# Four product groups of two Mish blocks made inside the pairs' stage before them

## The chip, the cores and the metric

The kernel runs on one core of a Trainium2 chip. The time is that of one launch on the device, in microseconds (us). A core has five engines that run side by side, each through its own list of instructions in order: TensorE (PE, matmuls, with its weight loads PEld), VectorE (DVE), ScalarE (ACT), GpSimd (POOL) and SyncE (SP, which here only issues DMAs). They wait for one another through semaphores.

## The reference

Attention with one added to the softmax's denominator, then a feed-forward layer with Mish:

```python
scores = scale * np.matmul(q, k.transpose(0, 1, 3, 2))      # (8, 12, 448, 448)
m = np.max(scores, axis=-1, keepdims=True)
e = np.exp(scores - m)
attn = e / (np.sum(e, axis=-1, keepdims=True) + np.exp(-m) + 1e-09)
attn_out = np.matmul(attn, v)                               # (8, 12, 448, 64)
x = attn_out.transpose(0, 2, 1, 3).reshape(3584, 768)
h = x @ w_in                                                # (3584, 2048)
sp = np.where(h > 20.0, h, np.log1p(np.exp(np.minimum(h, 20.0))))
g = h * np.tanh(sp)                                         # Mish
out = g @ w_out                                             # (3584, 768)
```

All inputs and the output are float32 in memory; the kernel computes with bfloat16 operands.

## The kernel before

Two heads make a *pair*, a batch has six pairs (`HP`), so there are 48, and three pairs make a *unit*. Units 0 and 1 (pairs 0 to 5, batch 0) run in a loop of their own (line 635). The loop at line 670 runs the units 2 to 15, and then four more rounds without attention. Each of its rounds has two parts:

- The **pairs' stage**, twelve steps `n`, four for each pair. A step makes two tiles of exponentials with row sums on ScalarE (`exps`, line 353), and then fills the three score tiles `sc_tiles` again: score matmuls on TensorE, then the negated row maximum on VectorE (`scores`, line 307). So the scores run three steps ahead of the exponentials. From unit 4 on, pieces of the second product (`mm2_part`, line 539) are laid between the steps. In units 2 and 3 there are none yet: TensorE transposes scores, spreads denominators, and at step 7 makes six matmuls on a constant tile (`keep_busy`, dummies, line 745), whose result nobody reads.
- The **Mish block**, eight groups `f`. Each group is six product matmuls x·w_in (`mm1_mish`, line 509) into one PSUM bank and a Mish on ScalarE into `gT`. The unit 2 block makes the groups 0 to 7 of batch 0, unit 3 the groups 8 to 15, and so on. ScalarE loads a table before the Mishes and again before the next exponentials. Between the groups, the next unit's q and k are transposed (`transpose_pair`) and taken out of PSUM (`evac_qk`), and after group 7 its first three scores are issued. These have to find their PSUM banks empty.

The product groups use the two banks `mo_tiles` in turn, and the third group of a block takes a half of `sc_tiles[0]`. The same two banks serve the spreads and the transposes on TensorE.

A pair's exponentials `en` go through these steps:

1. `denominators` (line 379): den and its reciprocal `rden` on VectorE, for the three pairs of a unit together, after a last small exponential `expm` of the maxima; for pairs 0 to 11 also a split of `rden` in two bfloat16 parts `hl` on GpSimd.
2. Either `normalise` divides `en` on VectorE (seven instructions, line 430; pairs from 12 on, `LATE_DIV`), or, for pairs 0 to 11, the division is made after the product with v: `spread_rden` (line 394) brings the reciprocals into a row layout by 16 small matmuls and a copy `rb`, and the result is multiplied by `rb` on its way from PSUM to `xT` (line 493).
3. `en` is transposed to `eT`, by a DMA that SyncE issues (line 438), or on TensorE (`turn_on_pe`, line 443) for the pairs 5, 6 and 7 (`BY_PE`) and for the last quarter of the first six.
4. `av_pair` (line 461) multiplies by v, into half a score tile, and its result goes to `xT[b]`, the operand of the product groups. `AV_AT` gives the steps for pairs 3 to 8; from pair 9 on the product of pair p lies ahead of the last scores of pair p + 3.

`RDEN_AT` says at which step of units 2, 3 and 4 a pair's denominators are spread. The matrices `w_in` (12 pieces) and `w_out` (8 pieces) are loaded by DMAs that GpSimd issues (`load_w`, line 160), at the steps in `W_AT` and at three places outside it. With `behind=p`, a small copy that reads pair p's `eT` goes ahead, so that GpSimd waits for that transpose. GpSimd also casts q, k and v (`cast`), in the same order of instructions.

For pairs from 12 on, q is laid out in two diagonal blocks (`q_diag`, four buffers), whose other halves are zeros. They are set once for each buffer, for pairs 12 to 15 (lines 264 and 265, VectorE).

The order of all this is written out by hand (`manual_schedule`): each engine runs its instructions in program order.

## Time and profile before

| | us |
|---|---|
| three runs | 473.57, 473.69, 466.44 |
| median of them | 473.57 |
| profiled execution, its time | 468.53 |
| profiled execution, its span (first to last instruction) | 466.8 |

| engine | busy us | share of the span | instructions |
|---|---|---|---|
| TensorE | 449.8 | 96% | 3051 |
| VectorE | 344.1 | 74% | 657 |
| ScalarE | 332.8 | 71% | 877 |
| GpSimd | 180.4 | 39% | 258 |

The mean granted TensorE clock of the profiled execution is 0.985 of full speed. The loop of units 0 and 1 ends near 46 us, units 2 and 3 take the time to 97.4 us, and all that comes after lasts to 466.8 us. A product matmul of 448 columns shows 352 ns from its start to its end, but starts follow each other faster than that, since matmuls are pipelined; where the cost of a row of them matters, it is read from the time that a whole group took.

How to read the lines below: each stands for one instruction, or for several of the same kind in a row (x8), with its start and length in us, its engine, the line of the kernel, and "what it writes<-what it reads". In square brackets is the time that the engine sat idle before, and what ended it.

### The profile page before, as it was taken

The numbers are of one execution on the slowest core, as the hardware profiler recorded it, in microseconds if no ns is written. First come the engines' busy times: TensorE is split into PE (matmuls) and PEld (weight loads), VectorE is DVE, ScalarE is ACT, GpSimd is POOL, SyncE is SP. The second block draws the span as 40 slices with busy tenths as digits, with TensorE's granted clock in tenths as the row PEclk, the third lists the DMA queues.
The fourth block names the chain that finished last, engine by engine and source line by source line (L and its number), as shares of the span: only waits on it lengthen the run. The fifth ranks groups of instructions, "written<-read, shape, count | busy, mean of one in ns | idle before, by whom it ended". The sixth has DMA issues, their size and how long they took to land.

```text
span 466.8 us, 8833 instructions
## 1 busy us (share of the span) xinstructions
PE 449.8 (96%) x3051; PEld 247.3 (53%) x3051; DVE 344.1 (74%) x657; ACT 332.8 (71%) x877; POOL 180.4 (39%) x258
## 2 busy tenths in 40 slices
PE   6988998999999999999999999999999999999996
PEld 3344555555655555555555555555555555556563
DVE  5889929669899898989897979988897979311021
ACT  5899878879787878788797878787878879211300
POOL 4523655104327173646464562727364610100000
PEclk8689999999999999999999999999999999999999
DMA  8999989999999999999999999999989493921122
GB/s 225 245 207 239 234 192 227 173 240 258 229 228 286 239 236 238 277 239 259 227 292 215 272 205 248 263 228 268 235 269 225 119 243 104 240 66 34 35 67 69
DMA packets 232493, 97.94 MB, mean 210 GB/s; under 512 B 189312, under 2 KB 228992, under 8 KB 232448
## 3 DMA queue, kind: packets, MB, share of 16 engines
q1 hardware_dynamic: 224928, 91.06, 83.6%
q0 software_dynamic: 7488, 6.29, 9.0%
q8 instruction: 24, 0.39, 0.4%
q14 instruction: 21, 0.17, 0.1%
q10 hardware_dynamic: 32, 0.02, 0.0%
HBM read 45.61 MB, written 11.01 MB: 121 GB/s over the span
## 4 chain that ended last, share of the span: by engine, by line
PE 76%; ACT 9%; DVE 9%; DMA 2%; issue 2%; SPq 1%; POOL 0%; DVEq 0%; ACTq 0%; POOLq 0%
PE mo L514 28%; PE mo L567 25%; PE sc L327 8%; ACT en L361 7%; PE sc L478 7%; DVE negm L348 6%; PE sc L514 4%; PE sc L288 1%; DMA v_f<-in_v_dram 1%; PE mo L288 1%; DVE eT L453 1%; PE sc L220 1%; DMA qT_all<-q_cast 1%; PE sc L333 1%; PE mo L478 1%
## 5 line engine op out<-in xcount | busy, mean ns | idle before, releaser
L361 ACT ACTIVATE en<-sc,negm 128x448 bf16<-128x448 f32 x336 | 208.8, 641 | 31.2 <-DVE negm L348 29.4
L348 DVE TENSOR_REDUCE negm<-sc 128x2 f32<-128x896 f32 x192 | 180.4, 969 | 43.1 <-PE sc L327 29.7
L567 PE MATMUL mo<-w_out_sb,gT 128*128 128x384 bf16 (+1 forms) x1024 | 166.7, 306 | 0.4 <-DVE rb L418 0.4
L514 PE MATMUL mo<-xT,w_in_sb 128*128 128x448 bf16 x672 | 134.4, 352 | 0.3 <-DVE xT L491 0.3
L567 PEld LDWEIGHTS <-gT 128*128 128x128 bf16 x1024 | 96.3, 98 | 56.0 <-issue 1.9
L268 POOL TENSOR_SCALAR qd<-qT_all 64x448 bf16<-64x448 bf16 x60 | 80.0, 1333 | 91.4 <-DMA qT_all<-q_cast 79.8
L514 PEld LDWEIGHTS <-w_in_sb 128*128 128x128 bf16 x768 | 74.4, 98 | 68.8 <-issue 3.0
L520 ACT ACTIVATE gT<-mo 128x448 bf16<-128x448 f32 x112 | 59.3, 543 | 70.1 <-PE mo L514 69.9
L430 DVE TENSOR_SCALAR en<-en,rden 128x448 bf16<-128x448 bf16 x252 | 82.3, 402 | 0.5
L361 ACT ACTIVATION_READ_ACCUMULATOR en<-sc,negm 128x1 f32 x336 | 71.2, 212 | 0.0
L550 DVE COPY o_sb<-mo 128x384 f32<-128x384 f32 (+1 forms) x64 | 31.9, 498 | 49.6 <-PE mo L567 48.8
L327 PE MATMUL sc<-kT_all,qd 128*128 128x448 bf16 x252 | 67.6, 354 | 0.0
L478 PE MATMUL sc<-eT,v_bf 112*64 112x448 bf16 x336 | 39.8, 357 | 1.2 <-ACT en L361 0.8
L327 PEld LDWEIGHTS <-qd 128*128 128x128 bf16 x252 | 24.6, 98 | 28.7 <-issue 12.9
L186 POOL CAST q_cast<-q_f 112x512 bf16<-112x512 f32 x47 | 28.6, 608 | 19.2 <-DMA q_f<-in_q_dram 18.9
L478 PEld LDWEIGHTS <-v_bf 112*64 112x64 bf16 x384 | 19.8, 109 | 19.9 <-issue 12.3
L186 POOL CAST v_bf<-v_f 112x512 bf16<-112x512 f32 x48 | 28.0, 605 | 2.7 <-DMA v_f<-in_v_dram 2.7
L186 POOL CAST k_cast<-k_f 112x512 bf16<-112x512 f32 x47 | 28.5, 607 | 1.0 <-DMA k_f<-in_k_dram 0.8
L714 POOL COPY marks<-en 1x2 bf16<-1x2 bf16 x12 | 2.1, 174 | 64.9 <-DVE en L430 64.9
L514 PE MATMUL sc<-xT,w_in_sb 128*128 128x448 bf16 x96 | 20.8, 352 | 0.0
L491 DVE CAST xT<-sc 128x448 bf16<-128x448 f32 x33 | 20.3, 615 | 0.0
L520 ACT ACT_TABLE_LOAD x14 | 18.0, 1283 | 0.8 <-PE mo L514 0.2
(63 smaller groups left out, 251.1 us busy)
## 6 DMA issues: line engine op xcount, KB each, us to landing
k_f<-in_k_dram SPq DMA_DIRECT2D x48, 224.0 KB, 5.0
q_f<-in_q_dram SPq DMA_DIRECT2D x48, 224.0 KB, 4.9
v_f<-in_v_dram SPq DMA_DIRECT2D x48, 224.0 KB, 5.1
w_in_sb<-in_moe_w_in_dram POOLq DMA_DIRECT2D x12, 256.0 KB, 9.1
w_out_sb<-in_moe_w_out_dram POOLq DMA_DIRECT2D x8, 384.0 KB, 12.0
out_dram<-o_sb SPq DMA_DIRECT2D x7, 336.0 KB, 3.4
out_dram<-o_sb SPq DMA_DIRECT2D x8, 288.0 KB, 5.1
out_dram<-o_sb SPq DMA_DIRECT2D x8, 240.0 KB, 3.6
```

What stands on the lines that cost most here:

```text
L186: nc.gpsimd.tensor_copy(out=to[nm], in_=src)
L268: q_reads.append(by.tensor_scalar(out=qd[rows, :, h, :], in0=q_ps[rows, 0:S].rearrange("d (i r) -> d i r", i=QB), scalar1=SCALE, scalar2=N ...
L327: nc.tensor.matmul(sc[:, bk, 0:S], lhsT=qT[:, i].rearrange("d h r -> d (h r)"), rhs=kT, start=True, stop=True,)
L348: half_max[p] = nc.vector.tensor_reduce(out=negm, in_=sc[:, 0 : len(cols), 0:S], axis=AX.X, op=ALU.max, negate=True)
L361: e = nc.scalar.activation(out=st["en"][:, :, c, 0:SP_], in_=sc[:, bk, 0:S].rearrange("q (j c) -> q j c", j=NT), func=AF.Exp, bias=st["neg ...
L430: nc.vector.tensor_scalar(out=en[:, :, i, 0:SP_], in0=en[:, :, i, 0:SP_], scalar1=st["rden"][:, i : i + 1], scalar2=None, op0=ALU.mult,)
L478: mm = nc.tensor.matmul(av[h * 64 : (h + 1) * 64, 0:S], lhsT=v_bf[:, h, j * D : (j + 1) * D], rhs=e_h, start=(j == 0), stop=(j == NT - 1),)
L491: read = nc.vector.tensor_copy(out=to, in_=av[:, 0:S])
L514: nc.tensor.matmul(h_ps[:, 0:S], lhsT=w_in_sb[:, dm, ff * 128 : (ff + 1) * 128], rhs=xT[b][:, dm, :], start=(dm == 0), stop=(dm == DM_T - 1),)
L520: nc.scalar.activation(out=gT[:, ff, b % 2 * S : b % 2 * S + S], in_=h_ps[:, 0:S], func=AF.Mish)
L550: nc.vector.tensor_copy(out=o_sb[:, cols.start : cols.start + n_dve], in_=st["o"][:, 0:n_dve])
L567: nc.tensor.matmul(st["o"][:, 0:n_cols], lhsT=gT[:, ff, i * 128 : (i + 1) * 128], rhs=w_out_sb[:, ff, cols], start=(ff == 0), stop=(ff == ...
```

## The change

1. **Products ahead.** In the pairs' stages of units 2 and 3, the first four groups of the block that follows are begun at the steps 6, 7, 9 and 10 (`mm1_begin`). In unit 2 the first takes four of its six matmuls there and the other three take five each, because the parts of `xT` from the pairs 4 and 5 come later; in unit 3 all six. The first two groups use the two `mo` banks, the next two the halves of `sc_tiles[0]`. `mm1_mish` adds the rest and applies Mish. The six dummies of step 7 are gone.
2. **Pairs 6, 7 and 9** are divided by VectorE (`EARLY_DIV`), so their spreads and the copies of them are gone, and the step from PSUM to `xT` is a plain copy. The spread of pair 5 moves from step 6 to step 5. In the block, `normalise` is called for two pairs at group 0 and for the third after group 1; in unit 3 the order of pairs is 10, 9, 11.
3. **Zeros.** Those of `q_diag` are set by GpSimd, at step 8 of units 3 and 4.
4. **Weights.** Six pieces go out in unit 1 behind the transpose of pair 4 (before: two in the second pair's turn, four at step 0 of unit 2), two at step 5 of unit 2, five in its block behind pair 8, three at step 1 of unit 3, four at the end of its block behind pair 11.
5. **expm** is made ahead of the last exponentials of a unit instead of behind them, in all units of the second loop.

```diff
+    EARLY_DIV = (HP, HP + 1, HP + UNIT_PAIRS)
+    def divided(p):
+        return p >= LATE_DIV or p in EARLY_DIV
...
-            if p < DIAG_FROM + len(q_diag):
-                nc.vector.memset(qd[0:64, :, 1, :], 0.0)
-                nc.vector.memset(qd[64:128, :, 0, :], 0.0)
...
+        if s == STEPS - 1 and p >= HP and p % UNIT_PAIRS == UNIT_PAIRS - 1:
+            w = st["whole"]
+            nc.scalar.activation(out=w["expm"], in_=w["negm"], func=AF.Exp)
         for bk, c in enumerate(cols):
...
-        elif s == STEPS - 1 and p % UNIT_PAIRS == UNIT_PAIRS - 1:
-            w = st["whole"]
-            nc.scalar.activation(out=w["expm"], in_=w["negm"], func=AF.Exp)
...
-        for i in range(NTILE if p >= LATE_DIV else 0):
+        for i in range(NTILE if divided(p) else 0):
...
-            if p >= LATE_DIV:
+            if divided(p):
                 read = nc.vector.tensor_copy(out=to, in_=av[:, 0:S])
...
-    def mm1_mish(b, ff):
-        flush_late()
-        spare = ff % FF_U == 2
-        h_ps = sc_tiles[0][:, 0, :] if spare else mo_take()
-        for dm in range(DM_T):
+    begun = {}
+
+    def mm1_begin(b, ff, upto):
+        bank = mm1_bank(ff)
+        begun[b, ff] = (bank, upto)
+        mm1(b, ff, bank, 0, upto)
+
+    def mm1_bank(ff, ahead=2):
+        at = ff % FF_U - 2
+        return sc_tiles[0][:, at, :] if 0 <= at < ahead else mo_take()
+
+    def mm1(b, ff, bank, lo, hi):
+        for dm in range(lo, hi):
             nc.tensor.matmul(
-                h_ps[:, 0:S],
+                bank[:, 0:S],
                 lhsT=w_in_sb[:, dm, ff * 128 : (ff + 1) * 128],
                 rhs=xT[b][:, dm, :],
                 start=(dm == 0), stop=(dm == DM_T - 1),
             )
+
+    def mm1_mish(b, ff):
+        flush_late()
+        at = ff % FF_U - 2
+        spare = 0 <= at < (2 if b == 0 else 1)
+        if (b, ff) in begun:
+            h_ps, lo = begun.pop((b, ff))
+        else:
+            h_ps, lo = mm1_bank(ff, 2 if b == 0 else 1), 0
+        mm1(b, ff, h_ps, lo, DM_T)
...
-    RDEN_AT = {0: {0: 3, 2: 4, 6: 5}, 1: {0: 8, 2: 6, 6: 7}, 2: {3: 10, 5: 11}}
-
-    W_AT = ({0: 4, 5: 1}, {1: 2, 3: 1, 5: 1, 7: 1, 9: 1}, {3: 1, 5: 1, 7: 2})
-    W_BEHIND = {(0, 0): HEAD - 2}
+    RDEN_AT = {0: {0: 3, 2: 4, 5: 5}, 1: {0: 8}, 2: {3: 10, 5: 11}}
+    MM1_AT, MM1_SHORT = (6, 7, 9, 10), (2, 1, 1, 1)
+
+    W_AT = ({5: 2}, {1: 3})
...
-            if s == 3 and p == 1:
-                load_w(2)
...
                 cast(p + 3, "qkv" if p + 3 < HEAD else "qk")
+                if p == HEAD - 1:
+                    load_w(6, behind=p - 1)
...
-            if early is not None and n == 7:
-                keep_busy(6, bank=mo_free[0])
+            if early is not None and n in MM1_AT:
+                dm = DM_T - (MM1_SHORT[MM1_AT.index(n)] if u == UNITS_PER_B else 0)
+                mm1_begin(0, (u - UNITS_PER_B) * FF_U + MM1_AT.index(n), dm)
...
+            if n == steps - 4 and nxt >= DIAG_FROM:
+                for p_ in range(nxt, min(nxt + UNIT_PAIRS, DIAG_FROM + len(q_diag))):
+                    qd = q_diag[p_ % len(q_diag)]
+                    nc.gpsimd.memset(qd[0:64, :, 1, :], 0.0)
+                    nc.gpsimd.memset(qd[64:128, :, 0, :], 0.0)
...
         todo = sorted(range(p0, nxt), key=lambda p: p in BY_PE)
+        if u == UNITS_PER_B + 1:
+            todo = [p0 + 1, p0, p0 + 2]
...
-                load_w(3, behind=p0 + 2)
+                load_w(5, behind=p0 + 2)
+            if u == UNITS_PER_B + 1 and f == FF_U - 1:
+                load_w(4, behind=p0 + 2)
...
-                for p in todo if p0 < LATE_DIV else todo[:1]:
+                for p in todo[:2] if p0 < LATE_DIV else todo[:1]:
                     normalise(p, dma=p not in BY_PE)
-            if f == 5 and u == UNITS_PER_B + 1:
-                spread_rden(p0, copy=nc.scalar.copy)
...
+            if f == 1 and p0 < LATE_DIV:
+                normalise(todo[2], dma=todo[2] not in BY_PE)
```

## The prediction

> **What bounds the kernel now.** I read the chain of waits in shares first, then busy time by stage, then the chain in order of time, then ScalarE and SyncE in order of time.
>
> The chain in shares says TensorE for the whole; the change touches only units 2 and 3, each a pairs' stage and a Mish block:
>
> ```profile
> PE 76%; ACT 9%; DVE 9%; DMA 2%; issue 2%; SPq 1%; POOL 0%; DVEq 0%; ACTq 0%; POOLq 0%
> ```
>
> Busy time in four stretches: pairs' stage and block of unit 2, then of unit 3 (length, then PE, PEld, DVE, ACT, POOL):
>
> ```profile
> 46.40:57.80 11.40, 10.56 (x117) 6.05 (x117) 10.94 (x16) 9.34 (x28) 8.19 (x15) 1.00 1.07 236
> 57.80:68.80 11.00, 11.00 (x81) 5.95 (x79) 2.54 (x7) 8.35 (x20) 4.68 (x10) 1.00 0.88 194
> 68.80:85.10 16.30, 14.84 (x167) 9.12 (x165) 15.87 (x22) 14.04 (x41) 7.57 (x12) 1.00 1.29 213
> 85.10:97.40 12.30, 12.30 (x96) 6.87 (x95) 5.48 (x17) 9.59 (x22) 2.09 (x5) 1.00 1.21 208
> ```
>
> The pairs' stages are VectorE's (10.94 of 11.40, 15.87 of 16.30), the blocks TensorE's. TensorE idles 0.84 + 1.46 = 2.3 us in the pairs' stages, none in the blocks.
>
> The chain in order of time gives pitches (start, length, what):
>
> ```profile
> 55.39 1.24 PE mo L288 x6
> 56.63 0.30 PE sc L341
> ...
> 57.82 2.38 PE mo L514 x12
> 60.19 0.40 PE sc L220 x8
> 60.59 1.14 PE sc L514 x6
> ...
> 92.96 0.63 PE mo L409 x16
> ```
>
> A product matmul costs 1.14/6 = 0.19 us, six dummies (L288) 1.24, eight transposes of q and k 0.40, one spread of the denominators (L409) 0.63. The group table's 352 ns for L514 is a latency and would double everything.
>
> ScalarE around the end of unit 2's block, and SyncE's issue of two of the score transposes:
>
> ```profile
> 68.23 0.54 ACT L520 ACTIVATE gT<-mo 128x448 bf16<-128x448 f32 x1 [0.59 <-PE mo L514]
> 68.79 1.28 ACT L361 ACT_TABLE_LOAD   x1
> 70.08 0.63 ACT L361 ACTIVATE en<-sc,negm 128x448 bf16<-128x448 f32 x1
> ...
> 59.35 3.59 SPq L438 DMA_TRANSPOSE eT<-en  x1
> ...
> 75.50 14.79 SPq L438 DMA_TRANSPOSE eT<-en  x1
> ```
>
> Each block ends product, Mish, table load, first exponential of the next stage (70.08; 98.34 after unit 3). I measure the change at those two marks. The transpose of pair 8 held SyncE 3.59 us, that of pair 9 14.79.
>
> **What goes.** Two times six dummies, 2.48 us, and the spreads of pairs 6, 7 and 9, 3 x 0.63 = 1.89: 4.4 us of TensorE work. With the 2.3 us of idle this is a floor: nothing here can win more than 6.7 us, unless later units change, where the chain is TensorE's (138.66 to 157.19 without a break) and its instructions are the same.
>
> **What moves.** 4 + 5 + 5 + 5 = 19 product matmuls into unit 2's pairs' stage, 24 into unit 3's, 43 x 0.19 = 8.2 us. That is no gain by itself: it pays where it fills the time in which TensorE waits for the exponentials.
>
> Unit 2: the four of step 6 start behind the scores at 54.6 (spread of pair 5 now a step earlier). Scores, five, scores at 56.95, A·V of pair 5 to 57.8, then 5 + 5 to 59.75. The last scores come 0.1 us later than now, under VectorE's reductions (busy to 57.7), so that exponentials still end near 59.2. ScalarE loads its table to 60.6, which no early product shortens. TensorE has 29 matmuls left: 5 x 0.19 + two transpose groups 0.8 = 61.5, where the Mish of group 0 (61.1) has freed its bank; then 24 x 0.19 + 0.4 = 66.5. Mish, load: the exponential at 68.4. Gain 1.7 us.
>
> Unit 3: VectorE-bound as before, so it ends 1.7 earlier, and 0.2 more because the copy of pair 7's spread (0.43 on ScalarE at 83.37) is gone: last exponential 84.9 instead of 86.7. TensorE, 24 matmuls done, ends at 85.9, transposes twice (86.7), waits 0.3 for the first Mish (table load 85.1 to 86.4, Mish to 86.9), then 24 x 0.19 + 0.4 = 91.95. Mish and load: 93.85 instead of 98.34. Gain 4.5 in all.
>
> **What is added.** VectorE divides pairs 6 and 7 in unit 2's block, pair 9 in unit 3's. Seven divisions take 1.81 us alone (114.35, unit 4) and 21 beside GpSimd's q copies 7.22 (140.71): 0.26 to 0.34 each. 14 of them are 3.6 to 4.8 us; from rden at 60.0, with 0.9 of q scaling, VectorE is done at 64.5 to 65.7, before the scores at 66.5. Hidden, with 0.8 left; without that cover each us would cost one. In unit 3, 1.81 + 1.6 of q scaling after 85.5 ends, but for the last transposes, before 89.
>
> The Trainium skill (SBUF — State Buffer, "Who interferes with whom") says that VectorE in a 2-port mode and GpSimd lock one another out for a whole instruction, which speaks against dividing beside GpSimd. The trace agrees (0.34 against 0.26), and both ends are under the cover.
>
> Zeros: eight memsets of 0.24 leave VectorE's idle time, gain nothing. On GpSimd the case has no 64x448 memset; the bounds are 0.2 us (its 128x128 memset) and 1.33 (its 64x448 q copy). Six are 1.2 to 8 us from step 8 of unit 3 in an idle GpSimd (77.9 to 87.7); I take 3, no cost. Queued behind them are only the small hi/lo casts at 87.7. VectorE beside them runs copies out of PSUM, which kept 614 to 615 ns whether GpSimd worked or not. Moving the small exponential ahead frees rden 0.26 us earlier in every unit, under TensorE's products: zero.
>
> Weights: six pieces now go out in unit 1 behind the mark on pair 4's transpose, which lands at 45.5, 0.72 us each on GpSimd to 50. Behind them wait the hi/lo casts of pair 5 (45.4, now 50; needed by a spread at about 52.8), then the casts of q, k, v (45.8, now 50.4; needed at 60) and the loads that wait for their buffers. All have room. Landing took 8.2 to 9.1 us there and 12.1 at most elsewhere: pieces 0, 1, 2 at 54.1, 54.8, 55.6, needed at 54.6, 55.0 and 56.3. At 12.1 TensorE would stand till 58.4, and the stage end about 2.5 late. Bounds 0 to 2.5; I take 0.2, as the nearest pieces are those of 47.6. The two pieces no longer sent at 18.6 may end pair 1's transpose earlier, but nothing in that stage waits for it: zero.
>
> Pair 9's transpose is the costliest doubt. Now it starts at 75.5; afterwards it waits for the division (87.1) and stands on SyncE behind pair 10's. Ahead of it, eight pieces leave between 64 and 73 and land until 89 to 92. A transpose beside such pieces held SyncE 8.81 us (two pieces, at 20.0) and 14.79 (four). Pair 10's, from 78, then ends at 88 to 92, pair 9's lands 5.5 later, 93.5 to 97.5, and TensorE wants it at 95.4 in unit 4, in order, with scores behind it. Cost 0 to 2 us, at worst some 17; I take 0.5, between the bounds, because pieces leave earlier than now. Behind it on SyncE: pair 11's transpose, the next loads (now 100.1, then 96 to 99.5), and on GpSimd the mark on pair 11 before four pieces and the casts, which have until 110.
>
> The Trainium skill (DMA: Bandwidth & Descriptors, "SWDGE vs HWDGE vs iDMA") has each engine take its queues in turn; by an even turn a transpose would take some 7 us, an estimate. The rows 8.81 and 14.79 differ, and decide.
>
> **Sum.** 4.5 - 0.2 - 0.5 = 3.8 us. Against the profiled execution, 468.53 (span 466.8 and 1.7 around it), that is 464.7 us. Three other runs gave 466.44 to 473.69, median 473.57: the profiled one is near the lower end.
>
> **Rivals.**
> - Only the dummies count: the moved products lengthen the pairs' stages by what they shorten the blocks (the spreads of unit 3 lie under VectorE's bound there). 2.5 us less 0.7 for the doubts: 466.7. For it: TensorE was 93% busy in unit 2's pairs' stage (10.56 of 11.40). Against: 10 products per unit stand behind the last scores, where VectorE no longer waits for TensorE.
> - Weights late at step 6: 2.3 us worse, 467. The landing times speak against it.
> - Slower: pair 9's transpose. It decides once it lands after 99.7, 4.3 us after it is wanted. If pair 10's takes 14.79, to 93, and pair 9's as long, to 107.8, and 4 more to land, TensorE stands 16.4 us: 480.4. For it: the row of 14.79. Against: the pieces have then landed, and the two next transposes took 5.3 and 4.3.
> - The change does nothing to the time: only if the early groups were not ahead in the queue; the order of TensorE's instructions shows them there.
>
> **Chances.** Forecast 0.62 (461 to 466), only removed work 0.13, late weights 0.07, late transpose 0.16 (467 to 480, 0.06 of it over 2%), nothing or something not seen 0.02. The range goes from 460 (the floor, 468.53 - 6.7 = 461.8, and most of the 2.1 us by which a run lay under the profiled one) to 471 (a transpose 6 us late). Two percent, 9.4 us, is about what a measurement of this kernel can tell from no change. The floor forbids it against the profiled execution; against the median, 464.1 is enough, which half the forecast (0.31) reaches, if the kernel before is measured there again, for which I give 0.7, since two of its three timed runs lie there: 0.22 faster. Slower 0.06 + 0.02, within 0.70.
>
> **What would show it.** First exponential of unit 3 near 68.4, of unit 4 near 93.9; products of group 0 to 3 between the scores, with no gap over 0.5 us ahead of them; VectorE's 14 divisions done by 65.7; pair 9's transpose issued by 92. Wrong if the A·V of pair 9 follows a gap of TensorE, if step 6 does, or if units 5 to 15 change length.

## The result, and the profile after

The changed kernel takes 466.5 us (median of 22 executions, 464.92 to 469.4), the kernel before beside it 473.11 (22 executions, 466.44 to 475.23). The ratio is 0.9942, 95% interval 0.9915 to 0.9969. The ratio leaves out executions more than 1.5% above a kernel's fastest, and so some of the long ones of the kernel before; the two medians alone would give 0.986. Of the 22 executions of the kernel before, 16 lie above 469.4 us, the highest of the changed kernel; such executions are called *long* below. The profiled execution took 465.31 us (span 463.5) against 468.53 (466.8).

The forecast of 464.7 us lies 1.8 us below the median and 0.6 below the profiled execution. It is nevertheless not right: of its two gains one did not happen, and another came that was not in the sum.

I divide both traces at ScalarE's table loads: the first of a block (for Mish) and the one at its end (for the exponentials). Lengths in us; the last columns are unit 4's block and unit 5's pairs' stage together, and the rest.

| | first load of unit 2's block | unit 2, block | unit 3, pairs | unit 3, block | unit 4, pairs | unit 4 block + unit 5 pairs | rest of the span |
|---|---|---|---|---|---|---|---|
| before | 59.45 | 9.34 | 18.32 | 9.94 | 16.75 | 26.35 | 326.61 |
| after | 58.16 | 9.48 | 17.90 | 7.59 | 16.80 | 26.95 | 326.62 |
| difference | -1.29 | +0.14 | -0.42 | -2.35 | +0.05 | +0.60 | 0 |

The sum is -3.27, the difference of the spans. I do not put the first column down to the change. TensorE ran at half its clock for two stretches at the start, of 10.2 and 3.4 us in the kernel before and of 3.4 and 3.4 in the changed one, and these lengths differ between executions of one kernel (a second profile of the kernel before has a single one, of 3.4). Two kernels of the experiments that have the new order of weights, and stretches of 10.2 and 3.4, reach the first load at 59.40 and 59.41 us, as the kernel before does. What is left to the change in these two executions is 2 us: unit 3 gives 2.8, unit 2 nothing, units 4 and 5 take 0.6.

The chain of waits in shares, after: TensorE has less of it, ScalarE more.

```profile
PE 71%; ACT 14%; DVE 11%; issue 2%; DMA 0%; SPq 0%; DVEq 0%; ACTq 0%
```

Busy time in four stretches after, pairs' stage and block of unit 2, then of unit 3 (length, then PE, PEld, DVE, ACT, POOL; at the end PEclk, DMA share, GB/s):

```profile
45.15:56.77 11.62, 11.12 (x119) 6.22 (x119) 11.03 (x16) 9.76 (x30) 8.91 (x16) 1.00 1.12 224
56.77:67.65 10.88, 9.51 (x72) 5.13 (x70) 5.98 (x21) 8.08 (x19) 2.88 (x7) 1.00 1.16 229
67.65:83.66 16.01, 14.80 (x140) 8.62 (x139) 15.77 (x22) 13.52 (x39) 11.36 (x20) 1.00 1.16 216
83.66:93.50 9.84, 9.30 (x68) 5.35 (x67) 5.78 (x18) 8.64 (x20) 0.52 (x2) 1.00 1.31 183
```

The block of unit 2 was TensorE's without a gap (11.00 of 11.00); now TensorE has 1.37 us of idle in it, though it has less to do. And the DMA share (the mean busy share of the 16 DMA engines) stands above 1 in all four. It stood at 1.07, 0.88, 1.29 and 1.21 in the stretches of the kernel before, in the lines that the prediction printed and did not use.

TensorE in unit 2's block, after, in order of time:

```profile
58.67 0.73 PE L525 MATMUL mo<-xT,w_in_sb 128*128 128x448 bf16 x3
59.24 0.36 PE L225 MATMUL sc<-ident,q_cast 112*128 112x112 bf16 x4
59.44 0.36 PE L225 MATMUL sc<-ident,k_cast 112*128 112x112 bf16 x4
59.63 0.35 PE L525 MATMUL sc<-xT,w_in_sb 128*128 128x448 bf16 x1
61.35 0.35 PE L525 MATMUL sc<-xT,w_in_sb 128*128 128x448 bf16 x1 [1.37 <-ACT gT L541]
```

The two single matmuls are the last of groups 2 and 3. They write the two halves of one score tile (`sc`). The matmul of group 3 (at 61.35) waits until ScalarE has read group 2 out of the other half (Mish at 60.73, 0.58 long), and TensorE's order leaves nothing to put in between.

ScalarE at the end of the two blocks, after, as shown for unit 2 of the kernel before:

```profile
67.08 0.54 ACT L541 ACTIVATE gT<-mo 128x448 bf16<-128x448 f32 x1 [0.59 <-PE mo L525]
67.64 1.28 ACT L366 ACT_TABLE_LOAD   x1
68.93 0.63 ACT L366 ACTIVATE en<-sc,negm 128x448 bf16<-128x448 f32 x1
...
92.56 0.54 ACT L541 ACTIVATE gT<-mo 128x448 bf16<-128x448 f32 x1 [0.59 <-PE mo L525]
93.13 1.28 ACT L366 ACT_TABLE_LOAD   x1
94.42 0.63 ACT L366 ACTIVATE en<-sc,negm 128x448 bf16<-128x448 f32 x1
```

68.93 and 94.42 look near the forecast 68.4 and 93.9, but 1.3 us of each come from the start.

SyncE's issue of the score transposes, after: first that of pair 8, then that of pair 10, which now goes ahead of pair 9's (89.84, 3.93 us).

```profile
58.17 4.85 SPq L440 DMA_TRANSPOSE eT<-en  x1
...
79.56 10.18 SPq L440 DMA_TRANSPOSE eT<-en  x1
```

Pair 9's is off SyncE at 93.77, and its data landed 6.0 us after its issue, near 95.8. TensorE's product of pair 9 with v (A·V) starts with no wait:

```profile
95.93 0.95 PE L480 MATMUL sc<-eT,v_bf 112*64 112x448 bf16 x8
```

In the traces in which TensorE does stand for a transpose, it goes on some 0.13 us after the data landed (in the first experiment, landing at 97.86, A·V at 98.00). So the transpose came just as it was wanted. That of pair 12, the first of the next unit, came late (one transpose: shortest/median/longest issue in ns and its start; us from issue to landing; then TensorE):

```profile
L440 SPq DMA_TRANSPOSE eT<-en x1: 7616/7616/7616, 112.4 to 112.4; - x1
DMA to landing us min/median/max: 11.1/11.1/11.1
...
123.64 0.95 PE L480 MATMUL sc<-eT,v_bf 112*64 112x448 bf16 x8 [0.52 <-ACT en L366]
```

Issued at 112.37, it landed at 123.5, and unit 5's first A·V starts 0.14 us later. The profile names ScalarE, but the landing is what came last. This wait is most of the 0.6 us lost in units 4 and 5.

### The profile page after: what moved, and what is told of

Its sections match the earlier page's. It is cut to its first block, busy times and chain, and to the rows that moved or that the text cites. A ratio compares the mean times of both kernels' runs of the same rounds, so it can differ in the third digit from the quotient of the medians.

```text
span 463.5 us, 8735 instructions
## 1 busy us (share of the span) xinstructions
PE 443.5 (96%) x2991; PEld 243.9 (53%) x2991; DVE 346.9 (75%) x670; ACT 331.4 (72%) x874; POOL 184.3 (40%) x267
## 3 DMA queue, kind: packets, MB, share of 16 engines
q1 hardware_dynamic: 224928, 91.06, 83.1%
## 4 chain that ended last, share of the span: by engine, by line
PE 71%; ACT 14%; DVE 11%; issue 2%; DMA 0%; SPq 0%; DVEq 0%; ACTq 0%
PE mo L525 26%; PE mo L588 24%; ACT en L366 11%; DVE negm L350 8%; PE sc L329 8%; PE sc L480 6%; PE sc L525 4%; PE sc L290 1%; DVE eT L455 1%; PE sc L335 1%; DVE xT L493 1%; PE mo L480 1%; ACT L541 1%; PE sc L225 1%; ACT kT_all L280 0%
## 5 line engine op out<-in xcount | busy, mean ns | idle before, releaser
L525 PE MATMUL mo<-xT,w_in_sb 128*128 128x448 bf16 x660 | 132.2, 352 | 1.0 <-ACT gT L541 0.5
L541 ACT ACTIVATE gT<-mo 128x448 bf16<-128x448 f32 x110 | 58.2, 543 | 68.9 <-PE mo L525 68.7
L432 DVE TENSOR_SCALAR en<-en,rden 128x448 bf16<-128x448 bf16 x273 | 87.1, 394 | 0.6
L480 PEld LDWEIGHTS <-v_bf 112*64 112x64 bf16 x384 | 20.1, 109 | 20.1 <-issue 12.6
L525 PE MATMUL sc<-xT,w_in_sb 128*128 128x448 bf16 x108 | 23.4, 353 | 1.4 <-ACT gT L541 1.4
L493 DVE CAST xT<-sc 128x448 bf16<-128x448 f32 x36 | 22.1, 615 | 0.0
```

Source lines behind the costliest of these rows:

```text
L432: nc.vector.tensor_scalar(out=en[:, :, i, 0:SP_], in0=en[:, :, i, 0:SP_], scalar1=st["rden"][:, i : i + 1], scalar2=None, op0=ALU.mult,)
L480: mm = nc.tensor.matmul(av[h * 64 : (h + 1) * 64, 0:S], lhsT=v_bf[:, h, j * D : (j + 1) * D], rhs=e_h, start=(j == 0), stop=(j == NT - 1),)
L493: read = nc.vector.tensor_copy(out=to, in_=av[:, 0:S])
L525: nc.tensor.matmul(bank[:, 0:S], lhsT=w_in_sb[:, dm, ff * 128 : (ff + 1) * 128], rhs=xT[b][:, dm, :], start=(dm == 0), stop=(dm == DM_T - 1),)
L541: nc.scalar.activation(out=gT[:, ff, b % 2 * S : b % 2 * S + S], in_=h_ps[:, 0:S], func=AF.Mish)
```

## The experiments

Medians are of 4 to 12 executions each, but for two single ones of the kernel before. The experiments ran in sets, each set on one chip with the kernel before beside it (medians 469.74 to 472.8, 466.4 to 467.4 at the low end). Ratios are to that kernel, with 95% intervals. The changed kernel was not run again in these sets, so a difference of under 1 us from its 466.5 is not settled. Lengths are those of the table above.

**One part at a time.** Four kernels: the changed kernel with group 3's last matmul issued ahead of the Mish of group 2; without the products ahead; without the early divisions; and the kernel before with nothing but the new weight schedule.

```diff
 # group 3 (in mm1_mish, ahead of the activation)
+        if at == 0 and (b, ff + 1) in begun:
+            bank, lo = begun[b, ff + 1]
+            mm1(b, ff + 1, bank, lo, DM_T)
+            begun[b, ff + 1] = (bank, DM_T)
 # no products ahead
-            if early is not None and n in MM1_AT:
...
+            if early is not None and n == 7:
+                keep_busy(6, bank=mo_free[0])
 # no early divisions
-    EARLY_DIV = (HP, HP + 1, HP + UNIT_PAIRS)
+    EARLY_DIV = ()
-    RDEN_AT = {0: {0: 3, 2: 4, 5: 5}, 1: {0: 8}, 2: {3: 10, 5: 11}}
+    RDEN_AT = {0: {0: 3, 2: 4, 5: 5}, 1: {0: 8, 2: 6, 5: 7}, 2: {3: 10, 5: 11}}
...
 # weights only (on the kernel before; the load_w calls as in the change)
-    W_AT = ({0: 4, 5: 1}, {1: 2, 3: 1, 5: 1, 7: 1, 9: 1}, {3: 1, 5: 1, 7: 2})
+    W_AT = ({5: 2}, {1: 3})
```

Group 3 earlier:

> The last product matmul of group 3 is issued, in program order, ahead of the Mish of group 2, which reads the other half of the same score tile; nothing is left out. Lengths are counted from the first dummy of unit 2's pairs' stage to the first exponential of unit 3 (23.71 us in the kernel before, 23.80 in the changed one), from there to that of unit 4 (28.26 and 25.49), and from there to the table load of unit 5's block (41.81 and 42.46). Theory: unit 2 won nothing because this matmul waited 1.37 us for that Mish; without the wait unit 2 takes 22.2 to 22.6 us and the time falls by some 1.3 us against the changed kernel. Rival: ScalarE's own row (last exponential, table load, Mishes, copies) bounds unit 2's block anyway; then it stays above 23.4 and the time stays the same.

No products ahead:

> The changed kernel without its products ahead: every group is made in the block, and the six dummies of step 7 are back. Theory: the products ahead are what shortened unit 3; without them its 28.26 us shrink only by the spread of pair 9 in the block, to about 27.6 (25.49 with them), unit 2 stays at 23.6 to 23.9, and the time is 2 us above the changed kernel. Rival: the removed dummies and spreads, or the divisions, made the gain; then unit 3 stays under 26.6.

No early divisions:

> The changed kernel with the spreads of pairs 6, 7 and 9 as in the kernel before (pair 7's a step earlier) and no early divisions. Theory: the division is worth the 0.63 us of pair 9's spread in unit 3's block and little else, so unit 3 takes 26.0 to 26.6 us instead of 25.49; and the 0.65 us that unit 4 lost go away, because the table load ahead of unit 5's exponentials then no longer waits for VectorE, so the time is within 0.5 us of the changed kernel. Rival 1: the divisions carry the gain, unit 3 above 27.5. Rival 2: unit 4's loss is something else, and its 42.46 stay.

Weights only:

> The kernel before with the changed kernel's order of weight loads alone. Theory: the weights were not late anywhere, so all three lengths are those of the kernel before within 0.3 us (23.71, 28.26, 41.81), and the time is the same. Rival: the order of the loads frees the score transposes and the timed runs of the kernel before (466.4 to 475.2) fall to those of the changed one (464.9 to 469.4).

| | median (range) | ratio | unit 2, block | unit 3, pairs | unit 3, block | unit 4, pairs | unit 4 block + unit 5 pairs |
|---|---|---|---|---|---|---|---|
| group 3 earlier | 468.2 (466.39 to 470.63) | 0.9982 (0.9948 to 1.0016) | 7.95 | 17.90 | 7.59 | 22.71 | 26.38 |
| no products ahead | 468.71 (467.61 to 469.79) | 0.9989 (0.9955 to 1.0024) | 10.42 | 17.91 | 10.42 | 16.75 | 26.37 |
| no early divisions | 466.37 (465.47 to 467.45) | 0.9940 (0.9910 to 0.9969) | 9.52 | 18.81 | 8.66 | 17.64 | 26.36 |
| weights only | 467.38 (466.32 to 468.94) | 0.9953 (0.9923 to 0.9982) | 9.32 | 18.34 | 9.93 | 16.75 | 26.36 |

The new weight schedule alone gives most of the measured change (ratio 0.9953, the whole change 0.9942) and has none of the long executions: the expected lengths came, the expected time did not, and the rival holds. The early divisions are worth nothing in the median (466.37 without, 466.5 with), though they shorten unit 3 by 0.91 us in the pairs' stage and 1.07 in the block, more than was expected of them; without them unit 4's stage is 0.84 us longer, with a wait of 0.82 us for pair 9's transpose.

Without the products ahead the blocks take 10.42 us, longer than in the kernel before (unit 3 together 28.3 us, 27.6 expected). This is not the price of the products alone. That kernel still puts group 3 into the second half of the score tile (before the change it had a bank of its own), and TensorE waits there for the Mish of group 2, 0.79 us in unit 2's block and 1.47 in unit 3's:

```profile
62.59 1.29 PE L525 MATMUL sc<-xT,w_in_sb 128*128 128x448 bf16 x6 [0.79 <-ACT gT L541]
```

Less that wait, unit 3's block would be some 9 us long, so that the products ahead are worth about 1.4 us there; this is an estimate.

The first kernel is a surprise: unit 2's block is 1.53 us shorter, as the wait says, and the kernel is 1.7 us *slower* in the median. Its loss lies in unit 4. TensorE there:

```profile
98.00 1.71 PE L480 MATMUL sc<-eT,v_bf 112*64 112x448 bf16 x8 [3.92 <-DMA eT<-en]
```

and SyncE with the transpose of pair 10, ahead of pair 9's:

```profile
77.70 13.44 SPq L440 DMA_TRANSPOSE eT<-en  x1
```

The A·V of pair 9 wants its transpose 1.9 us earlier than in the changed kernel, and gets it 2 us later. TensorE's clock is half for 6.8 us, from 2 us into this wait on; these eight matmuls take 1.71 us, not 0.95. The page's row of the granted clock has it as the one 7 in the middle:

```profile
PEclk9899999979999999999999999999999999999999
```

**The weights back, pair 9 first, and a table load.** In the changed kernel the table load at the end of unit 4's block waits 1.08 us for VectorE, which it does not before. One theory (D) was that the 0.6 us lost in units 4 and 5 come from that. Four kernels: the old weight schedule in the changed kernel; group 3 earlier with pair 9 as before the change (not divided, first on SyncE); a single-element exponential behind unit 4's last Mish, to give the load an owner that does not wait; and the last two together.

```diff
 # pair 9 first (beside group 3 earlier)
-    EARLY_DIV = (HP, HP + 1, HP + UNIT_PAIRS)
+    EARLY_DIV = (HP, HP + 1)
-            todo = [p0 + 1, p0, p0 + 2]
+            todo = [p0, p0 + 1, p0 + 2]
+            if f == 5 and u == UNITS_PER_B + 1:
+                spread_rden(p0, copy=nc.scalar.copy)
 # table load
-    marks = singles.tile([1, 4, 16], BF16)
+    marks = singles.tile([1, 4, 8], BF16)
+    tiny = singles.tile([1, 8], FP32, tag="tiny", name="tiny")
...
+            if u == UNITS_PER_B + 2 and f == FF_U - 1:
+                nc.scalar.activation(out=tiny[:, 0:1], in_=ident[0:1, 0:1], func=AF.Exp)
```

Weights back:

> The changed kernel with the weight schedule of the kernel before (two pieces at pair 1, four behind the mark on pair 4 in unit 2, single pieces in units 2, 3 and 4); all else as changed. Theory A, that the weights' new places are what takes the runs of 470 to 478 us away (the kernel before has 21 of 35 there, the kernel with the new weight schedule alone none of 12, 466.32 to 468.94): the median goes to 468 to 472 and at least a third of the runs lie above 469.5. Theory B, that the products ahead and the divisions take them away: median 466 to 467.5, no run over 469.5. In the trace both expect the table load of unit 4's block end still to wait about 1.1 us for VectorE.

It gave 470.11 us (465.38 to 475.79), ratio 0.9982 (0.9933 to 1.003): theory A holds, with seven of twelve above 469.5. In its trace TensorE waits 4.33 us for pair 9's transpose, and unit 4's pairs' stage is 22.33 us long.

Pair 9 first:

> The kernel with the last matmul of group 3 ahead of the Mish of group 2, and pair 9 again as before: not divided early, its transpose the first of unit 3's three on SyncE, its spread (0.63 us) back in unit 3's block. Theory C, that pair 9's transpose stood in a bad place (in the run without this, TensorE waited 3.92 us for it, and then ran 6.8 us at half the clock): no wait of TensorE for a transpose at unit 4's first A.V, exponential load of unit 2's block end near 65.8 to 66.5, of unit 3's near 92, unit 4's pairs' stage back from 22.7 to 16.8 us: median 464 to 465.5. Rival, that the three transposes together are limited by what the 16 DMA engines move, whatever their order: SyncE is done with the three at 97.5 to 100 again, TensorE waits there for one of them 1 to 4 us, and the median is 466 to 468.5.

468.56 us (465.72 to 471.53), ratio 0.9993 (0.9958 to 1.0029): theory C is right on unit 4 and fell on the time; the rival's wait came, one unit further on than it said. Unit 4's stage is 16.75 us and has no wait, but SyncE holds the first transpose 17.66 us and is done with the three at 102.4, and TensorE waits 3.51 us for a transpose at unit 5's first A·V (127.12), again with 6.8 us of half the clock (from 126.07). Unit 4's block and unit 5's stage take 32.69 us together.

Table load, and both:

> The changed kernel with one exponential of a single element on ScalarE behind the last Mish of unit 4's block, so that the table load that follows belongs to it and not to the exponentials of the scores. Theory D, that the 1.08 us for which that load waited are on the path: table load at its old distance, 9.4 us from the block's first table load instead of 10.45, everything behind it 0.9 to 1.1 us earlier: median 465.4 to 465.7, ratio to the changed kernel 0.998. Rival, that VectorE's last reductions set the end of that block, and the load only stood beside it: load earlier, first exponential at the same time, median 466.5 as now.

> The two edits of the last two kernels together (group 3's last matmul ahead of the Mish of group 2, pair 9 as before the change, and the single exponential behind unit 4's last Mish). If theories C and D hold both: median 463 to 464.5, below the changed kernel's 466.5. If the transposes are limited by the DMA engines: what is gained ahead of unit 4 is waited for there, 465.5 to 467.5.

Neither answers its question: 483.62 us (ratio 1.031, 1.0253 to 1.0368) and 481.33 (1.0287, 1.0217 to 1.0357). From unit 5's block on, which the edit does not touch, the span is 12.6 and 7.8 us longer. In both, the two small tiles together are 96 bytes where the tile for the marks had been 128, so that all tiles made after them lie 32 bytes lower in SBUF.

**The place of the tiles, and the kernel before once more.** The same exponential with the two tiles adding up to the old 128 bytes; the changed kernel with nothing but the tile of 96; and two more profiles of the kernel before.

```diff
 # in place
+    marks = singles.tile([1, 4, 8], BF16)
+    tiny = singles.tile([1, 16], FP32, tag="tiny", name="tiny")
 # 32 bytes lower
+    marks = singles.tile([1, 4, 12], BF16)
```

> As the earlier kernel with one single-element exponential behind unit 4's last Mish, but with the two small tiles cut so that together they take the 128 bytes a partition that the one took before: no other tile moves in SBUF. If it was the move by 32 bytes that lengthened units 5 to 15 there (17.0 to 19.6 us from one block's table load to the next, against 16.8 to 17.1 in the changed kernel), they are back at 16.8 to 17.1, and theory D can be read: table load 9.4 us behind the block's first, first exponential 0.9 us earlier than in the changed kernel, median 465.4 to 465.7. If a wait for a transpose comes next in unit 5, as it did at 127.1 us in the kernel with pair 9 as before, median 466 to 468. If the single exponential itself was the cause, the later units stay long and the time is again 480 to 485.

467.25 us (466.08 to 468.79), ratio 0.9925 (0.9887 to 0.9964): theory D fell, and the time is the one expected with a wait for a transpose in unit 5. ScalarE behind unit 4's block:

```profile
121.45 0.54 ACT L542 ACTIVATE gT<-mo 128x448 bf16<-128x448 f32 x1 [0.59 <-PE mo L526]
122.02 1.28 ACT L796 ACT_TABLE_LOAD   x1
123.31 0.20 ACT L796 ACTIVATE tiny<-ident 1x1 f32<-1x1 bf16 x1
123.42 0.61 ACT L367 ACTIVATE en<-sc,negm 128x448 bf16<-128x448 f32 x1
```

The wait is gone and the first exponential comes 0.95 us sooner behind the Mish (1.43 instead of 2.38), but nothing follows from it. The second products start 9.75 us behind the block's first table load with it and without it, as TensorE sets that block; unit 4's block and unit 5's stage together are 27.75 us, against 26.95 in the changed kernel and 26.35 to 26.38 in seven other traces, four of which have the waiting load. What takes the 0.5 to 1.3 us there is a wait of TensorE at unit 5's first A·V. The profile puts it down to ScalarE, but pair 12's transpose, issued at 115.07, landed 11.9 us later, at 127.02, and the A·V starts at 127.15: it is the transpose, as in the changed kernel. The same run has 2.65 us of wait at unit 4's first A·V, where its order is that of the changed kernel: the transpose that came just in time there came late here.

> The changed kernel with nothing changed but the small tile for the marks, 96 bytes a partition in place of 128, so that every tile made after it stands 32 bytes lower in SBUF. If the place of the tiles is what cost 3% in the two kernels with the single exponential: 479 to 486 us, the divisions of seven again 0.49 us each in the later units instead of 0.405, the share of the 16 DMA engines taken by queue 1 at 90% instead of 83%. If it isn't: 465 to 469.

483.5 us (481.13 to 483.89), ratio 1.0254 (1.0186 to 1.0322): the place of the tiles is the cause of the long times. The transposes of the scores between 200 and 380 us (number; shortest/median/longest issue in ns; first and last start), first the changed kernel:

```profile
L440 SPq DMA_TRANSPOSE eT<-en x23: 3458/3574/4742, 195.5 to 375.7; - x23
```

and 32 bytes lower:

```profile
L440 SPq DMA_TRANSPOSE eT<-en x21: 4142/4788/7099, 200.8 to 373.3; - x21
```

A third more for each, with the same packets and bytes; TensorE waits for six of them there, 7.6 us in all. VectorE's divisions are longer too, 476 ns in the mean instead of 405 in the same stretch. No run separates the two, and none shows why 32 bytes matter.

> The kernel before once more, for a trace of one of its long executions (21 of 35 lie above 470). Theory A: if this one is above 469.5, TensorE waits 2 us or more for a transpose of the scores at an A.V of unit 4 or 5, a stretch at half the clock follows, and that unit's pairs' stage is 3 to 7 us longer than the 16.75 of the first trace; if it is below 469, no such wait. Rival: the lengths are those of the first trace and the time is lost ahead of unit 2 (half the clock at the start) or spread over all units.

> The kernel before a third time, for the same question, with the same expectations: above 469.5 with a wait of TensorE for a transpose of 2 us or more in unit 4 or 5 and a unit longer by 3 to 7 us, below 469 without; or, by the rival, lengths as in the first trace and the loss ahead of unit 2 or everywhere.

These took 472.1 and 473.04 us, two of the long executions. Of theory A the transpose came, with a wait of 1.98 and 2.75 us at unit 5's first A·V. The stretch at half the clock did not come in either, the units are 2.1 and 2.8 us longer and not 3 to 7, and there are waits that it had not named. TensorE in the second:

```profile
59.08 1.69 PE L514 MATMUL mo<-xT,w_in_sb 128*128 128x448 bf16 x8 [0.40 <-DMA w_in_sb<-in_moe_w_in_dram]
...
130.31 0.95 PE L478 MATMUL sc<-eT,v_bf 112*64 112x448 bf16 x8 [2.75 <-DMA eT<-en]
...
156.58 0.95 PE L478 MATMUL sc<-eT,v_bf 112*64 112x448 bf16 x8 [0.90 <-DMA eT<-en]
```

The waits are for weights in unit 2 and for transposes in units 5 and 6. The lengths say the same: against the first profile of that kernel, unit 2's block +0.57, unit 4's block and unit 5's stage +2.83, later +1.06, together 4.5 us, which is the difference of the spans (471.2 and 466.8). In the other: +1.32, +2.06 and +0.72, less 0.54 at the start, 3.6. Pair 12's transpose held SyncE 11.16 us here and 6.53 in the first profile. In the old schedule four pieces of weights go out at 106 to 111 us, just ahead of it; in the new one they go at 99 to 102. That this moves pair 12's transpose is argued from the times; the two experiments on the schedule show only what it does to the whole.

**Less to move.** To see whether it is the volume in front of the transposes, two kernels leave out the four pieces of w_out's first half (1.5 MB) and multiply by w_in in their place, so that their output is not the reference's.

```diff
-        for h in range(2):
+        for h in range(1, 2):
...
-                    rhs=w_out_sb[:, ff, cols],
+                    rhs=w_out_sb[:, ff, cols] if cols.start >= NH else w_in_sb[:, ff % DM_T, cols],
...
-    W_AT = ({5: 2}, {1: 3})
+    W_AT = ({5: 2}, {})
-                load_w(5, behind=p0 + 2)
+                load_w(4, behind=p0 + 2)
```

> The kernel with the last matmul of group 3 ahead of the Mish of group 2, without the four pieces of w_out's first half (1.5 MB, sent at 70 to 75 us): the second products take their weights for those columns from w_in, so that the output is not the reference's there. Volume theory (what a stage gains is lost where a transpose of the scores comes late, because the 16 DMA engines are busy all the time and the pieces stand ahead of it): the first transpose of unit 3 holds SyncE 5 to 9 us instead of 13.4, no wait of TensorE at unit 4's first A.V (3.92 us with the pieces), unit 4's pairs' stage 16.8 us instead of 22.7, no half clock there; profiled time 462 to 463.5, median 462.5 to 464. Rival (the transposes have a pace of their own that the pieces do not change): first transpose 12 us or more again, TensorE waits 3 to 4 us, median 467 to 469.

> The changed kernel without the same four pieces of w_out (the second products take w_in there, the output is not the reference's). Volume theory: in the profiled run of the changed kernel pair 9's transpose landed just in time, so that only the executions in which it lands late gain: median 465 to 466, highest below 468 (469.4 with the pieces), and the kernel with the early matmul of group 3 is now 1.5 to 2 us faster than this one, where it was 1.7 slower. Rival: 466.5 as before, the other kernel still slower.

With group 3 earlier 462.87 us (462.49 to 463.59), ratio 0.9893 (0.9852 to 0.9933); without it 464.97 (463.97 to 465.89), ratio 0.9933 (0.9901 to 0.9966). SyncE in the first:

```profile
77.40 5.37 SPq L440 DMA_TRANSPOSE eT<-en  x1
...
85.82 3.54 SPq L440 DMA_TRANSPOSE eT<-en  x1
```

13.44 us have become 5.37; pair 9's transpose is off SyncE at 89.4, 4.3 us before TensorE wants it (93.71), and unit 4's stage is back at 16.75. Now the edit that had cost 1.7 us of median gains 2.1; in the two traces 2.0, of them 1.54 in unit 2's block, 0.31 in unit 5 and 0.2 at the start. The volume theory holds in all but two numbers, which it missed by 0.1 us at most (the second kernel's median, 464.97 for 465 to 466, and the gain of 2.1 for 1.5 to 2). The DMA share says the same; in the stretch of unit 3's block, with the pieces and without:

```profile
82.00:91.50 9.50, 8.96 (x66) 5.18 (x65) 5.49 (x17) 8.30 (x20) 0.52 (x2) 1.00 1.32 165
82.00:91.50 9.50, 8.96 (x66) 5.14 (x64) 5.48 (x17) 8.29 (x19) 0.52 (x2) 1.00 0.84 183
```

**Three loads later, with everything computed.** Three loads that are wanted only in unit 4 (q and k of pair 15, v of pair 12; 0.67 MB) moved on SyncE behind unit 3's transposes, with and without group 3 earlier.

```diff
+                if (u, n) != (UNITS_PER_B + 1, LOAD_AT[2]):
-                load_pair(at + LEAD, "qk")
-                load_pair(at + 1, "v")
+                    load_pair(at + LEAD, "qk")
+                    load_pair(at + 1, "v")
...
                 load_w(4, behind=p0 + 2)
+                load_pair(p0 + 2 + LEAD, "qk")
+                load_pair(p0 + UNIT_PAIRS, "v")
```

> The kernel with the last matmul of group 3 ahead of the Mish of group 2, all weights loaded, and three loads (q and k of pair 15, v of pair 12; 0.67 MB, sent at 72 to 73.2 us, wanted by GpSimd's casts in unit 4) moved on SyncE behind unit 3's three transposes. Volume theory: 0.67 of the 1.5 MB that freed the transpose in the last kernel is gone from in front of it, some 2.5 to 3 us of the 16 engines at 230 to 250 GB/s; TensorE's wait at unit 4's first A.V falls from 3.92 to 0 to 1.5 us, and the median to 463.5 to 466, below the changed kernel's 466.5. Against it: the loads now stand in front of pair 12's transpose (116 us), and a wait there at unit 5's first A.V gives it back: 466 to 468.5.

> The changed kernel with the same three loads moved behind unit 3's transposes, as the control. Volume theory: pair 9's transpose lands with room, the executions of 468 to 469.4 go, median 465 to 466. If the loads collide with pair 12's transpose instead, 466.5 to 468.

467.47 us (465.8 to 469.59), ratio 0.9901 (0.9867 to 0.9935), and 466.61 (464.63 to 468.45), ratio 0.9903 (0.9866 to 0.994). Unit 4's wait is gone with group 3 earlier and 0.23 us without (its stage 16.75 and 17.05), and unit 5's first A·V waits in both, 1.74 and 2.31 us, until 0.13 us after pair 12's transpose landed. So the medians are those expected for that case. With group 3 earlier:

```profile
124.51 0.76 PE L480 MATMUL sc<-eT,v_bf 112*64 112x448 bf16 x6 [1.74 <-DMA eT<-en]
```

The loss moves on by one unit. No kernel here that computes everything is shown to beat the changed one: the lowest median is that without early divisions (466.37 against 466.5), and the two lowest ratios, 0.9901 and 0.9903 in this set, have intervals that overlap its 0.9942 (0.9915 to 0.9969).

## Why the prediction was right in unit 3 and wrong in the whole

**What bounds the kernel.** "The pairs' stages are VectorE's, the blocks TensorE's" holds for the order inside a unit. Across units 2 to 5 there is a third bound, which was in the lines shown: the 16 DMA engines, with a share of 0.88 to 1.29. The prediction treated transfers one by one, each as late or in time, and not as a queue that a faster TensorE runs into.

**Unit 2, 1.7 us: failed.** The step is "TensorE has 29 matmuls left: 5 x 0.19 + two transpose groups 0.8 = 61.5, where the Mish of group 0 (61.1) has freed its bank". It asked only for the bank of group 0 and missed that groups 2 and 3 share a score tile. The block took 9.48 us instead of 7.8. With the wait taken away it took 7.95, so the rest of that working was right. But the step would not have paid even so: the 1.5 us came back as 5.9 us more in unit 4's stage, because pair 9's transpose could come no sooner. Without the four pieces in front of it, the 1.5 us stayed.

**Unit 3, 2.8 us: right.** 0.42 us in the pairs' stage (0.2 booked there) and 2.35 in the block, whose end came 7.59 us behind its table load (7.5 worked out). The kernel without early divisions, with 8.66 us for the block, shows their part of it. The kernel without products ahead, with 10.42, shows that they are needed, but not their size, because 1.47 us of it are the score tile's wait.

**Weights, 0.2 us of cost: wrong in sign for the median.** In the profiled execution nothing waits for them, and none of the feared 2.5 us came; the products of step 6 run on without a gap:

```profile
53.38 0.93 PE L525 MATMUL mo<-xT,w_in_sb 128*128 128x448 bf16 x4
```

A wait for weights in that stage came only in the three kernels with the tiles 32 bytes lower (1.30 to 2.03 us). What the sum did not have is the kernel before's long executions. Their waits for weights and transposes cost 3.6 and 4.5 us in the two that were profiled, and the new schedule takes most of them away: 467.38 us against 471.28 with the weights alone, and 470.11 against 466.5 when they are put back. This is more of the measured gain than the products and divisions together, whose own part (467.38 to 466.5) is not clear of the noise. The prediction saw the spread (466.44 to 473.69) and used it only to judge the chances, though its rows of 8.81 and 14.79 us for a transpose beside pieces of weights, against 3.59 for another, show how far such a transfer can run late. It also read the landing of pieces as 12.1 us at most; that holds for w_in, and pieces of w_out took up to 15.8.

**Pair 9's transpose, 0.5 us: mechanism right, size too small.** In the profiled execution it cost nothing, landing as it was wanted, which is luck. Over all executions the volume in front of the transposes costs the changed kernel some 1.5 us of median (466.5 against 464.97 without the four pieces, in another set), pair 12's included. Pair 12's was not in the sum; its wait is the 0.52 us in unit 5. The rival of 480 us did not come: the pieces had landed, as was argued against it, and pair 9's transpose took 3.93 us (of the two transposes named there, 5.3 and 4.3, the first is 5.16 in the trace). What it had not reckoned with is the half clock behind a wait: with 3.92 us of wait, unit 4's stage is 5.9 us longer.

**Divisions and zeros: right.** VectorE was done with the 14 divisions at 62.7 (65.7 at the latest expected), and a memset of 64x448 took GpSimd 0.46 to 0.49 us, some 3 us for six; that the 3 us taken were met is luck, between bounds of 1.2 and 8. The small exponential was not tested by itself. The division has a side effect that was not seen: the table load of unit 4's block now waits 1.08 us (not in the kernel without early divisions); it lies beside TensorE's work.

**The sum.** 465.31 us were profiled against the 464.7 of the forecast, but with 1.29 us that came at the start, ahead of the change's gains. Without these it would have been 466.6, about the time of the rival "only the dummies count" (466.7), though not by its way. That the forecast lies near is luck: a gain of 1.7 us missing, 0.6 lost in units 4 and 5, and 1.29 from the start. The range held; the chance of 0.62 for the forecast's mechanism was too high.

## What to carry to other kernels

A wait that is removed is worth what the next resource allows: before booking it, read the DMA share of that stretch, and how long before its use each transfer lands. Where that margin was nil here, sending something later moved the loss to the next unit, and only less volume freed it. Two halves of one tile can wait for each other; look for the tile, not for the bank. And a kernel whose executions spread over 2% may have waits that come in some of them, as here: profile a long one before predicting.

## What was not expected of the hardware

- **32 bytes of place.** With the tiles behind a small one made 32 bytes shorter, issue of a transpose went from 3.57 to 4.79 us, the DMA engines' time on that queue from 83.1% to 90.2% of the span, and the kernel from 466.5 to 483.5. The Trainium skill (DMA: Bandwidth & Descriptors, "Constraints") asks for 32-byte alignment in SBUF for a DMA transpose; a move by 32 bytes keeps that, and still costs a third. The account in the Trainium skill, on the same page, that reads split at 256-byte boundaries ("How a descriptor splits into AXI transactions") would fit; no run here shows which boundary counts.
- **Half the clock after a wait.** Every wait of TensorE of 3.0 to 4.3 us (five traces) brought 3.4 or 6.8 us at a granted clock of 0.5, beginning between 2 us into the wait and 1 us behind it; of the shorter ones two for weights did (1.71 and 2.03 us), but not those of 2.65 to 2.82 for transposes. In each trace the changes of the clock lie whole multiples of 3.413 us apart. Cut into windows on that grid, from 45 us to 20 us before the end, the traces sort themselves: the five windows with 2.05 to 3.41 us of idle TensorE were followed by half the clock, those at full clock with up to 1.90 us were not, but for the two with the waits for weights (1.57 and 1.71 us). The waits of 2.65 to 2.82 us fell across two windows. The Trainium skill (TensorE: Matmul & The Clock Gate, "What's actually happening") has windows of 3.4 us that run freely, of which an idle one halves the clock; the lengths agree, but here a window that was idle for 2.05 of its 3.41 us was enough.
- **One instruction's issue.** The first transpose of unit 3 held SyncE from 10.06 to 17.80 us in kernels with all weights, and 5.37 and 4.37 without four pieces of them. Its data landed 2.0 to 5.0 us after SyncE was done with it.
